# Pooled attention and a GELU MLP on one core: a step's loads placed behind its softmax transposes

## The chip, the cores and the metric

The kernel runs on one core of a Trainium2 chip. The metric is the device time of one execution in microseconds (us). The engines have names in the profile: PE is TensorE (matrix products; PEld is its loading of weights), DVE is VectorE, ACT is ScalarE, POOL is GpSimd, and SP is SyncE, which here issues nearly all DMAs.

## The reference

Inputs are q, k, v of shape (8 batches, 8 heads, 576 positions, 64) in float32, and two weight matrices.

```python
k_p = k.reshape(B, H, 72, 8, D).mean(axis=3)     # v_p likewise: eight positions pooled to one
scores = q @ k_p.T / sqrt(D)                     # softmax over the 72 pooled positions
attn_out = softmax(scores) @ v_p
x = attn_out as (4608 tokens, 512)
h = x @ w_in                                     # 512 -> 2048
out = gelu_tanh(h) @ w_out                       # 2048 -> 512
```

## The kernel before, in words

The tokens are worked in nine groups. Groups 0 to 7 are the first 512 positions of each batch; group R (number 8) holds the last 64 positions of all eight batches and runs in the last place but one (`seq` is 0 to 6, R, 7). The weights are put into SBUF once, as bf16.

A prologue computes the attention of group 0, then the MLP of group 0 runs (`mlp_first`). After that there is one step for each further group, numbered n_ from 1 to 8. In step n_ TensorE runs the MLP of group g = seq[n_], and between its matmuls stands the attention of the next group, seq[n_+1]. The MLP has a hidden part (16 blocks of four 128x512 matmuls at L421 and L360, each followed by a Gelu on ScalarE at L424 and L362) and an output part (seven products of a Strassen form, 112 matmuls of 256 columns at L472). Four PSUM banks with the tag `mm` take the hidden blocks in turn. VectorE prepares sums of the Gelu outputs for the products (`g_sums`, L411 to L414).

The order is written out by hand. `at(hooks, s, f, ...)` puts a call at place s of the step's matmuls; the call is made before that matmul in program order. Places 0 to 63 are the hidden part, 64 to 175 the output part. Each engine runs its own instructions in program order and waits only for its data and buffers, so for SyncE a place says only what stands before and after a DMA in its queue.

For the attention of the next group, these are the pieces that the change and the prediction speak of:

- `load_kv` loads K (1 MB, L108, and a half chunk at L103), a half chunk of V (L101) and then V (1 MB, L108) into one of two `kv` buffers; its `parts` choose K with the half chunks (0) or V (1). `load_q` loads the queries of a group (1 MB, L120) into one of two `q_sb` buffers; for group R it loads 64 rows of each batch into `q_r` (L124), two batches a call.
- `pool` sums eight positions on VectorE (L147 to L149). `k_transpose_dma` transposes the pooled keys through a DMA (kTd from kvb, L199), and `k_spread` copies the result into a block form on VectorE (kbd from kTd, L90). `spread_v` does a like thing for the values on GpSimd (L169).
- `cast_q` makes bf16 queries (q_b), and `q_transpose_dma` transposes them through a DMA (qT, L220). `cast_gated` does the casts on GpSimd behind a small copy from `eb`, which holds them back until the softmax weights of the step are written.
- `scores` (L236) at places 68 and 94, `exps` on ScalarE (L245), `norm` on VectorE, once on GpSimd (L252 to L267), and for each of four quarters an `e_transpose_dma` (eT from eb, L294) follow. `values` (L326; L335 for group R) at place 64 + 105 needs all four eT and gives the xT of the next step's MLP.
- `store_pair` writes half of a group's output (512 KB, L392) after the sixth and the seventh product.

In step n_ before the change, SyncE has, in order: kTd, the loads of K and V for the group two ahead, the q of that group, in steps 2 to 5 a part of group R's queries, four eT, a store, qT of the group two ahead, a store. Step 1 differs: its q for group 3 and K for group 3 are loaded at places 44 and 45, and V at 64 + 52, behind the fourth eT.

Of the kernel before, what the change touches and what calls it, by code (L numbers as in the profile page):

```python
# [19 lines left out]
def kernel(  # L20
# [21 lines left out]
    nc = tc.nc  # L42
# [10 lines left out]
    R = B  # L53
    seq = list(range(B - 1)) + [R, B - 1]
# [55 lines left out]
    def q_tile(g):  # L110
        if g < B:
            st[g]["q"] = work.tile([128, H, 4, D], F32, name="q_sb")
        else:
            st[g]["q"] = consts.tile([128, H, 4, D], F32, name="q_r")

    def load_q(g, j0, j1, eng):
        t = st[g]["q"]
        if g < B:
            src = q[g, :, :MAIN, :].rearrange("h (p j) d -> p h j d", j=4)
            eng.dma_start(out=t[:, :, j0:j1], in_=src[:, :, j0:j1])  # L120
        else:
            for b in range(2 * j0, 2 * j1):
                p0 = 64 * (b % 2)
                eng.dma_start(out=t[p0:p0 + 64, :, b // 2, :], in_=q[b, :, MAIN:, :].rearrange("h t d -> t h d"))  # L124
# [532 lines left out]
    def at(hooks, s, f, *a):  # L657
        hooks.setdefault(s, []).append(lambda: f(*a))
# [6 lines left out]
    hooks = {}  # L665
# [44 lines left out]
    for n_, g in enumerate(seq):  # L710
        if n_ == 0:
            continue
        hooks = {}
        if n_ == 1:
            for i in range(1, 4):
                at(hooks, i, w_sums, i, 0, NP, nc.vector)
            at(hooks, 36, g_sums, 0, 4)
        else:
            at(hooks, 20, g_sums, 0, 2)
            at(hooks, 36, g_sums, 2, 4)  # L720
        at(hooks, 57, g_sums, 4, 6)
        at(hooks, 65, g_sums, 6, 8)
        if n_ + 1 < len(seq):
            n = seq[n_ + 1]
            b = B - 1 if n == R else n
            kv = n != B - 1
            if n_ == 1:
                for j in range(4):
                    at(hooks, 28 + 4 * j, cast_q, n, j, j + 1, nc.scalar)
                at(hooks, 41, qT_tile, n)  # L730
                at(hooks, 41, q_transpose_dma, n)
            if kv:
                t0 = 22 if n_ == 1 else 12
                at(hooks, t0, pool, b, 0, 5)
                at(hooks, t0, dup_k, b, 0, 5)
                at(hooks, t0, kT_tile, b, None)
                at(hooks, t0, k_transpose_dma, b)
                t1 = t0 + (16 if n_ == 1 else 24)
                at(hooks, t1, pool, b, 5, 9)
                at(hooks, t1, spread_v, b, nc.gpsimd)  # L740
                at(hooks, 56, k_spread, b, [nc.vector, nc.vector])
            for j in range(4):
                if j % 2 == 0:
                    for f in (scores, exps):
                        for i in (j, j + 1):
                            at(hooks, 64 + (4 if j == 0 else 30), f, n, i)
                if j == 0:
                    at(hooks, 64 + 17, eT_tile, n)
                nj = 64 + [17, 33, 40, 50][j]
                at(hooks, nj, norm, n, j, nc.gpsimd if j == 1 else nc.vector)  # L750
                at(hooks, nj, e_transpose_dma, n, j)
            at(hooks, 64 + 66, nc.scalar.preload_act_table_set, GELU_SET)
            at(hooks, 64 + 105, xT_tile, n)
            at(hooks, 64 + 105, values, n, [nc.scalar, nc.vector])
        if n_ + 2 < len(seq):
            n2 = seq[n_ + 2]
            if n2 != R:
                s2 = 44 if n_ == 1 else 57
                at(hooks, s2, q_tile, n2)
                at(hooks, s2, load_q, n2, 0, 4, nc.sync)  # L760
            at(hooks, 64 + 52, cast_gated, n2)
            at(hooks, 64 + 100, qT_tile, n2)
            at(hooks, 64 + 100, q_transpose_dma, n2)
            if n_ == 1:
                at(hooks, 45, load_kv, n2, (0,))
                at(hooks, 64 + 52, load_kv, n2, (1,))
            else:
                at(hooks, 28, load_kv, n2)
        if n_ == 1:
            at(hooks, 58, q_tile, R)  # L770
        if 2 <= n_ <= 5:
            at(hooks, 58, load_q, R, n_ - 2, n_ - 1, nc.sync)
        mlp(g, hooks, n_ + 1 == len(seq))


# [28 lines left out]
```

The softmax here doesn't subtract the row's maximum and nothing guards it: scores larger than these inputs give would overflow.

## Time and profile before

| | us |
|---|---|
| median of 3 runs (284.69 to 285.91) | 285.53 |
| the profiled execution | 289.0 |
| its span, from the first to the last instruction | 287.3 |
| TensorE busy in that span | 276.0 |
| VectorE, ScalarE, GpSimd busy | 200.2, 168.2, 58.1 |

| step (by its hidden part's first matmul, L421) | starts at, us |
|---|---|
| 1 | 52.3 |
| 2 | 82.7 |
| 3 | 113.3 |
| 4 | 142.9 |
| 5, 6, 7, 8 | 171.3, 199.7, 228.8, 257.0 |

The times in a line of the profile are in us from the start of the span unless it says ns. A timeline's line gives the start, the length, the engine, the source line, the operation and the tiles written and read (`out<-in`), how many instructions are merged, and in brackets the idle time of the engine before the first of them with what ended it. A line of the windows view gives a stretch, its length, the busy time and count of instructions for PE, PEld, DVE, ACT and POOL, and at the end the granted TensorE clock (1 is full), the busy share of the DMA engines and GB/s. "DMA to landing" is the time from the start of the issuing instruction to the arrival of the data.

### The profile page before, as it was taken

To read this page: it belongs to the slowest core of one execution; us is meant where nothing else is said; L and a number is where in the kernel's file an instruction comes from. 1 tells how busy PE (TensorE), PEld (TensorE's weight loads), DVE (VectorE), ACT (ScalarE), POOL (GpSimd) and SP (SyncE) were. 2 spreads that over 40 slices of the span, in tenths; PEclk is the share of its full clock that TensorE was granted. 3 is DMA by queue.
4 is the path that set the end of the run, shared out by engine and by line. 5 is a ranking of instruction groups with operands and counts; after the bars stand their busy time and mean duration, and the time that the engine had idled before them with its cause. 6 is when DMAs were issued, how large, how long until landed. Compare 5 with 4: busy or idle time off the path is not lost.

```text
span 287.3 us, 6029 instructions
## 1 busy us (share of the span) xinstructions
PE 276.0 (96%) x2430; PEld 176.4 (61%) x2430; DVE 200.2 (70%) x361; ACT 168.2 (59%) x264; POOL 58.1 (20%) x91
## 2 busy tenths in 40 slices
PE   8889999998989997999999999999999999999994
PEld 3678844446844683448745864586458845864583
DVE  4882868987867984499679966996699435844521
ACT  1586574787446852676467646763776377637620
POOL 4740272002400340031203120312031200100000
PEclk9999999999999998999999999999999999999999
DMA  7999999999989998696689868946813730253013
GB/s 227 303 186 281 373 385 179 325 328 258 197 236 255 308 175 192 216 347 73 157 221 349 131 158 222 283 55 154 235 48 43 168 104 0 48 119 75 1 40 111
DMA packets 71759, 54.34 MB, mean 189 GB/s; under 512 B 45618, under 2 KB 57906, under 8 KB 71730
## 3 DMA queue, kind: packets, MB, share of 16 engines
q1 hardware_dynamic: 69474, 51.72, 70.2%
q0 software_dynamic: 2112, 2.10, 4.6%
q8 instruction: 19, 0.31, 0.5%
q10 hardware_dynamic: 144, 0.13, 0.1%
q14 instruction: 10, 0.08, 0.1%
HBM read 36.70 MB, written 9.44 MB: 161 GB/s over the span
## 4 chain that ended last, share of the span: by engine, by line
PE 78%; DMA 4%; DVE 3%; issue 1%
PE mm L360 32%; PE mm L472 31%; PE mm L421 5%; PE xo L326 3%; PE x L472 2%; DMA eT<-eb 2%; PE sc L236 2%; DMA qT<-q_b 2%; DVE eb L267 1%; DVE den L252 1%; PE xo L335 1%; PE mm L376 0%; DVE r L261 0%; DVE kv L147 0%; DVE kv L148 0%
## 5 line engine op out<-in xcount | busy, mean ns | idle before, releaser
L360 PE MATMUL mm<-xT,w_in_b 128*128 128x512 bf16 x448 | 98.0, 379 | 0.0
L362 ACT ACTIVATE gT<-mm 128x512 bf16<-128x512 f32 x112 | 66.9, 598 | 27.8 <-PE mm L360 27.7
L360 PEld LDWEIGHTS <-w_in_b 128*128 128x128 bf16 x448 | 43.7, 98 | 52.9
L472 PEld LDWEIGHTS <-gT 128*128 128x128 bf16 x512 | 48.5, 98 | 10.4 <-issue 2.5
L169 POOL TENSOR_TENSOR vbd<-kvb,vmask 128x256 bf16<-128x256 bf16 (+2 forms) x40 | 23.0, 597 | 96.6 <-DVE kvb L149 55.7
L472 PEld LDWEIGHTS <-stage 128*128 128x128 bf16 x384 | 37.5, 98 | 4.4
L411 DVE TENSOR_TENSOR stage<-gT 128x512 bf16<-128x512 bf16 (+1 forms) x31 | 15.6, 503 | 21.4 <-ACT gT L362 21.2
L472 PE MATMUL mm<-tw,gT 128*128 128x256 bf16 x240 | 30.4, 276 | 0.0
L472 PE MATMUL mm<-w_out_b,gT 128*128 128x256 bf16 x240 | 29.9, 273 | 0.0
L88 ACT CAST xT<-xo 128x1024 bf16<-128x1024 f32 (+1 forms) x11 | 10.2, 935 | 32.7 <-PE xo L326 28.0
L252 DVE TENSOR_REDUCE den<-e 128x8 f32<-128x576 f32 x36 | 26.5, 736 | 3.2 <-ACT e L245 2.9
L88 ACT COPY osb<-mm 128x512 f32<-128x512 f32 x30 | 17.6, 588 | 17.3 <-PE mm L472 17.0
L472 PE MATMUL mm<-tw,stage 128*128 128x256 bf16 x224 | 26.7, 273 | 0.0
L147 DVE TENSOR_TENSOR kv<-kv 128x1024 f32<-128x1024 f32 (+3 forms) x19 | 21.3, 1119 | 7.6 <-DMA kv<-in_k_dram 5.1
L245 ACT ACTIVATE e<-sc 128x576 f32<-128x576 f32 x36 | 21.8, 649 | 6.0 <-PE sc L236 4.4
L267 DVE TENSOR_TENSOR eb<-e,r 128x576 bf16<-128x576 f32 x25 | 20.8, 831 | 0.9
L412 DVE TENSOR_TENSOR gT<-gT 128x512 bf16<-128x512 bf16 (+1 forms) x31 | 14.6, 470 | 8.9 <-ACT gT L362 7.6
L90 DVE CAST xT<-xo 128x1024 bf16<-128x1024 f32 (+1 forms) x9 | 10.0, 1106 | 15.0 <-PE xo L326 11.4
L267 POOL TENSOR_TENSOR eb<-e,r 128x576 bf16<-128x576 f32 x7 | 8.1, 1150 | 56.5 <-ACT e L245 56.5
L90 POOL CAST q_b<-q_sb 128x1024 bf16<-128x1024 f32 (+1 forms) x13 | 13.6, 1067 | 20.1 <-DMA q_sb<-in_q_dram 20.0
L421 PE MATMUL mm<-xT,w_in_b 128*128 128x512 bf16 x64 | 16.3, 400 | 0.1
L371 PE MATMUL mm<-xT,w_in_b 128*128 128x256 bf16 x128 | 15.6, 273 | 0.1
(84 smaller groups left out, 288.9 us busy)
## 6 DMA issues: line engine op xcount, KB each, us to landing
kv<-in_k_dram SPq DMA_DIRECT2D x7, 1024.0 KB, 6.7
q_sb<-in_q_dram SPq DMA_DIRECT2D x7, 1024.0 KB, 11.3
kv<-in_v_dram SPq DMA_DIRECT2D x6, 1024.0 KB, 9.4
out_dram<-osb SPq DMA_DIRECT2D x12, 512.0 KB, 3.0
kv<-in_v_dram SPq DMA_DIRECT2D x4, 512.0 KB, 10.8
w_in_b<-in_moe_w_in_dram POOLq DMA_DIRECT2D x4, 512.0 KB, 6.7
w_out_s<-in_moe_w_out_dram SPq DMA_DIRECT2D x2, 1024.0 KB, 13.7
stage<-in_moe_w_out_dram SPq DMA_DIRECT2D x2, 1024.0 KB, 14.9
```

The source lines that it names most:

```text
L88: eng.copy(out=out, in_=in_)
L90: eng.tensor_copy(out=out, in_=in_)
L147: add(out=t[:, :, 0:4, :], in0=t[:, :, 0:4, :], in1=t[:, :, 4:8, :], op=ALU.add)
L169: eng.tensor_tensor(out=vbd[p0:128, b, n0:n1, :].rearrange("p (c r) (hh d) -> p c (r hh) d", c=max(m, 1), d=D), in0=kvb[p0:128, 4 + c0:4 + ...
L245: nc.scalar.activation(out=e.rearrange("p (x h) s -> p x (h s)", x=2), in_=sc[:, :, 0:4 * Sp], func=ACT.Exp, scale=1.0 / 64.0)
L252: nc.vector.reduce_sum(out=den, in_=e, axis=AX.X)
L267: eng.tensor_tensor(out=o.rearrange("p (pr hh s) -> p hh pr s", hh=2, s=Sp), in0=e.rearrange("p (hh pr) s -> p hh pr s", hh=2), in1=r.rear ...
L360: nc.tensor.matmul(out=hp, lhsT=w_in_b[:, ko, fo * 128:(fo + 1) * 128], rhs=st[g]["xT"][:, ko, :], start=(i == 0), stop=(i == KO - 1))
L362: nc.scalar.activation(out=gT[:, fo, :], in_=hp, func=ACT.Gelu_apprx_tanh)
L371: nc.tensor.matmul(out=hp[:, f, :], lhsT=w_in_b[:, ko, (fo + f) * 128:(fo + f + 1) * 128], rhs=st[g]["xT"][:, ko, c0:c0 + 256], start=(ko ...
L421: nc.tensor.matmul(out=hp[f], lhsT=w_in_b[:, ko, f * 128:(f + 1) * 128], rhs=st[g]["xT"][:, ko, :], start=(ko == 0), stop=(ko == 3))
L472: nc.tensor.matmul(out=xs[p] if acc is xs else acc[:, p, :], lhsT=lt, rhs=rt, start=bool(fresh and m == 0 and (p == 0 or (last and acc is ...
```

## The change

In each step the loads are placed behind the fourth eT (place 64 + 50) instead of ahead of the first. V is loaded for the group two ahead, as before, at place 64 + 53. K with the half chunks and q are loaded at 64 + 54 for the group three ahead, one group further than before. Group R's queries move to the same place and begin one step earlier, in steps 1 to 4. In step 1, K for group 3 stays at place 45, and q for group 3 moves from place 44 to 64 + 53. The queries of group 3 are cast in step 2 by ScalarE at places 16, 20, 24 and 28 and transposed at 29; before, GpSimd cast them in step 1 and they were transposed at its place 64 + 100. Later groups are cast and transposed where they were. SyncE then has in a step: kTd, four eT, V, K and half chunks, q, a part of group R's queries, a store, qT, a store.

```diff
-            if n_ == 1:
+            if n_ <= 2:
+                s0 = 28 if n_ == 1 else 16
                 for j in range(4):
-                    at(hooks, 28 + 4 * j, cast_q, n, j, j + 1, nc.scalar)
-                at(hooks, 41, qT_tile, n)
-                at(hooks, 41, q_transpose_dma, n)
+                    at(hooks, s0 + 4 * j, cast_q, n, j, j + 1, nc.scalar)
+                at(hooks, s0 + 13, qT_tile, n)
+                at(hooks, s0 + 13, q_transpose_dma, n)
...
+        def load_q_of(n):
+            q_tile(n)
+            load_q(n, 0, 4, nc.sync)
+
+        if n_ == 1:
+            at(hooks, 45, load_kv, seq[3], (0,))
         if n_ + 2 < len(seq):
             n2 = seq[n_ + 2]
-            if n2 != R:
-                s2 = 44 if n_ == 1 else 57
-                at(hooks, s2, q_tile, n2)
-                at(hooks, s2, load_q, n2, 0, 4, nc.sync)
-            at(hooks, 64 + 52, cast_gated, n2)
-            at(hooks, 64 + 100, qT_tile, n2)
-            at(hooks, 64 + 100, q_transpose_dma, n2)
+            at(hooks, 64 + 53, load_kv, n2, (1,))
             if n_ == 1:
-                at(hooks, 45, load_kv, n2, (0,))
-                at(hooks, 64 + 52, load_kv, n2, (1,))
+                at(hooks, 64 + 53, load_q_of, n2)
             else:
-                at(hooks, 28, load_kv, n2)
+                at(hooks, 64 + 52, cast_gated, n2)
+                at(hooks, 64 + 100, qT_tile, n2)
+                at(hooks, 64 + 100, q_transpose_dma, n2)
+        if n_ + 3 < len(seq):
+            n3 = seq[n_ + 3]
+            at(hooks, 64 + 54, load_kv, n3, (0,))
+            if n3 != R:
+                at(hooks, 64 + 54, load_q_of, n3)
         if n_ == 1:
-            at(hooks, 58, q_tile, R)
-        if 2 <= n_ <= 5:
-            at(hooks, 58, load_q, R, n_ - 2, n_ - 1, nc.sync)
+            at(hooks, 64 + 54, q_tile, R)
+        if 1 <= n_ <= 4:
+            at(hooks, 64 + 54, load_q, R, n_ - 1, n_, nc.sync)
```

## The prediction

> **What bounds the kernel now.** First the page: TensorE is busy nearly all the span, so only what makes it wait can move the time. Then TensorE's timeline in the steps that the diff touches. In its lines the number in brackets is the idle time before a group.
>
> ```profile
> PE 276.0 (96%) x2430; PEld 176.4 (61%) x2430; DVE 200.2 (70%) x361; ACT 168.2 (59%) x264; POOL 58.1 (20%) x91
> ```
>
> ```profile
> 67.51 0.46 PE L236 MATMUL sc<-kbd,qT 64*64 64x72 bf16 x32 [0.82 <-DMA qT<-q_b]
> ...
> 80.60 1.18 PE L326 MATMUL xo<-eT,vbd 32*64 32x512 bf16 x16 [1.02 <-issue]
> ...
> 110.87 1.18 PE L326 MATMUL xo<-eT,vbd 32*64 32x512 bf16 x16 [1.77 <-issue]
> ```
>
> From step 1 on these are the only holes: 0.82 us in step 1 (scores wait for the transposed queries), 1.02 at its end and 1.77 at the end of step 2 (the values wait for transposed softmax weights, eT). From step 3 on a step takes 28.4 us without a hole. After the third hole the windows view shows a second loss:
>
> ```profile
> 108.90:110.90 2.00, 0.23 (x6) 0.06 (x5) 0.00 (x0) 0.00 (x0) 0.00 (x0) 1.00 0.67 166
> 110.90:113.00 2.10, 2.10 (x22) 1.03 (x23) 0.89 (x1) 1.01 (x1) 0.00 (x0) 0.82 1.02 256
> 113.00:116.00 3.00, 3.00 (x11) 1.18 (x9) 2.93 (x4) 0.65 (x2) 0.00 (x0) 0.56 0.97 259
> ```
>
> The clock (third number from the end) falls to 0.82 and 0.56; the eight L421 matmuls take 2.88 us instead of 1.89 and the seven L472 before them 1.40 instead of 0.87, so 1.5 us are lost.
>
> Why eT is late is in SyncE's timeline, which issues nearly all DMAs in one order:
>
> ```profile
> 88.04 1.48 SPq L199 DMA_TRANSPOSE kTd<-kvb  x1
> 89.57 0.57 SPq L108 DMA_DIRECT2D kv<-in_k_dram  x1
> ...
> 92.04 0.51 SPq L120 DMA_DIRECT2D q_sb<-in_q_dram  x1
> 92.59 5.05 SPq L124 DMA_DIRECT2D q_r<-in_q_dram  x2
> 101.15 8.18 SPq L294 DMA_TRANSPOSE eT<-eb  x4
> ...
> 141.11 3.23 SPq L220 DMA_TRANSPOSE qT<-q_b  x1
> 144.44 0.54 SPq L392 DMA_DIRECT2D out_dram<-osb  x1
> 146.35 1.20 SPq L199 DMA_TRANSPOSE kTd<-kvb  x1
> ```
>
> The first eT of step 2 is issued at 101.15 and lands 6.1 us later, at 107.3, just after the rest queries (q_r, 106.7): it queued behind the step's loads. The kTd of 146.35, with nothing but a store ahead, lands in 2.6 us:
>
> ```profile
> L294 SPq DMA_TRANSPOSE eT<-eb x1: 3572/3572/3572, 101.2 to 101.2; - x1
> ...
> DMA to landing us min/median/max: 6.1/6.1/6.1
> ```
>
> ```profile
> L199 SPq DMA_TRANSPOSE kTd<-kvb x1: 1202/1202/1202, 146.4 to 146.4; - x1
> ...
> DMA to landing us min/median/max: 2.6/2.6/2.6
> ```
>
> **The Trainium skill.** "DMA: Bandwidth & Descriptors", section Queues, rings and completion order: a DMA engine takes the descriptors of one queue in ring order. The trace agrees (6.1 against 2.6 us). "TensorE: Matmul & The Clock Gate", section What's actually happening: the array's clock is halved after an idle window of some 3.4 us. The trace's clock record has half speed for 3.41 us from 112.24, and 1.77 us of idling inside a window was enough; 1.02 was not. The same page's table of the array calls ScalarE's queue strictly in order: a cast that waits holds back every Gelu behind it. No wait of this kind is in the trace before.
>
> **The change part by part.** All bytes and all DMAs stay; they move on SyncE's queue.
>
> *Off the path of eT.* In step 1 the 1 MB of q for group 3 no longer stands before eT. The K load then lands some 3 us earlier than 75.3, so the second eT (issued 74.29, taking 2.10) takes its usual 1.2 to 1.6, and the last one lands near 79.6 instead of 80.40: the hole of 1.02 goes. In step 2 nothing stands before eT: the third hole, 1.77, goes, and with it the half clock, 1.5. The 0.82 stays, as nothing before it moves. Profiled 289.0 (span 287.3 plus 1.7 around it) − 1.02 − 1.77 − 1.5 = **284.7**. The median, 285.53, lies 3.5 below the profiled execution, so the timed runs hardly pay these losses, and the gain against the median is at most about 0.8.
>
> *GpSimd and ScalarE.* Group 3's gate and two casts leave GpSimd (0.19 + 2 × 1.04 us; it is 20% busy: nothing). Four casts of 0.6 us go to ScalarE between Gelus of step 2. Step 1 has the same four at 59.0 to 62.6 and TensorE ran on through them, as four PSUM banks lie between: 0 in themselves. Their wait for q is counted below.
>
> *In the way of kTd and qT.* Behind the last eT now come, in one block, V, K with two half chunks, q and q_r, and only then store, qT, store and kTd (in step 2: both stores, kTd, qT). Before, the latter four came first. Scores need kTd, then k_spread on VectorE (0.93 us), and qT. Call X the start of the values matmuls; the last eT is issued 2.75 before, V 1.45 before, and scores of the next step are due at X + 16.4 (140.86 to 157.28).
>
> Two bounds on the block. *Lower*, by the packet records (median 84 ns for 2 KB, 46 for 1 KB, 18 for 256 B, 159 for 4 KB, over 16 engines): V 32 × 84 = 2.7 us, K with halves 40 × 84 = 3.4, q 64 × 46 = 2.9, q_r 64 × 18 = 1.2, a store 8 × 159 = 1.3, qT 128 × 18 = 2.3, kTd 40 × 18 = 0.7; data begins 2 us after the issue, and landing comes about 0.9 after the last packet. *Upper*, by the distance from one landing to the next in a full queue: the first V 6.8 after its issue, K 3.3, halves 1.2, q 3.9, q_r 1.0, store 1.3, qT 2.5, kTd 0.7 (K at 124.25 to q_r at 133.46 in step 3 is such a chain).
>
> - Steps 3 and 4 (3.5 MB loaded in the step before). Lower: X + 0.5 + 15.8 + 0.9 = X + 17.2, with k_spread 18.1: TensorE waits 1.7. Upper: 5.4 (V), 9.9 (K), 13.8 (q), 14.8, 16.1, 18.6, 19.9, 20.6 (kTd), 21.5: it waits 5.1. I take two thirds of the way up, since the mean packet (106 ns for 2 KB) is well over the median: 4.0 each, **8.0**.
> - Step 2 (4.5 MB; q of group 3 too). V issued about 78.2. Lower: 80.2 + 18.7 + 0.9 = 99.8; upper: 85.1, q3 89.0, K 93.5, q4 97.4, 98.4, stores 101.0, kTd 101.7, qT 104.2. Scores would be due at 96.1 (97.02 less the hole). Wait 3.7 to 8.1, taken **6.6**. ScalarE's casts, due about 85.5, wait for q3 until 87 to 89; the Gelus behind stall, the banks cover 3.5 us, and what is left (0 to 2.5) lies inside this wait, for qT comes later still.
> - Step 5 (2.5 MB, no q): 0 to 1.2, taken **0.8**. Step 6 (V and q alone): scores in time, VectorE late by up to 1.6; taken **0.3**.
> - What follows each wait of steps 2 to 4: an idle time above 1.77 should halve the clock again, 1.5 as measured. Should it not, VectorE is late instead: it waits in k_spread, then has eight sums of 0.46, so the softmax starts 3.75 after scores instead of 2.26 (97.02 to 99.28), and eT, which had 0.1 to spare in step 3 (landed 140.7, needed 140.8), comes 0.9 or more late. The one covers the other: 1.5 each, **4.5** (2.7 to 5.1).
>
> Sum: 284.7 + 8.0 + 6.6 + 0.8 + 0.3 + 4.5 = **304.9**; all lower ends 294.5, all upper ends 310. As the timed runs pay less for late transfers than the profiled one, I take **303**.
>
> **Rivals.**
> *Not slower: the block drains in time.* If transposes pass the loads, or the 3.5 MB land so fast that kTd lands before X + 15.5, only the holes go: 284.7, or 283.9 with the first hole gone too. For: the DMA engines are 0.72 to 0.87 busy in the windows of steps 4 and 5, so there is room over a step. Against: even the lower bound misses that point by 1.7, and every eT behind loads landed behind them. Chance 0.07.
> *Only ScalarE's wait.* kTd is in time, but the casts of step 2 hold TensorE for 1.3 to 2.5: 286 to 287. Chance 0.05.
> *Only step 2.* 4.5 MB are too much and 3.5 MB just fit: 284.7 + 3.7 + 1.5 = 290. Chance 0.08.
> *That the order isn't moved* is excluded: SyncE's list of instructions has V, K, q and q_r after the four eT in each step.
> The main case, waits for kTd in steps 2 to 4: 0.80.
>
> **Numbers.** Within 0.5% (1.4 us) is what a measurement of this kernel can tell from no change. Faster by more: 0.04, the larger part of the rival that drains in time (its first hole gone too). Same: 0.06, the rest of it (0.03) and of the second rival 0.03. Slower: 0.90, the main case, the third rival and the second's last 0.02. The main case's range is 294 to 310; to hold the time 8 times in 10 beside the third rival it reaches down to 292.
>
> **What would show it.** Right: in the profile after, TensorE's idle time before L236 in steps 2, 3 and 4 of several us, released by kTd or qT (k_spread on VectorE, the copy kbd<-kTd at L90, waiting for DMA kTd); kTd landing 9 us or more after its issue where it took 2.6; no idle time before L326 in steps 1 and 2; clock below 1 after each wait. Wrong: kTd landing in under 4 us, steps 3 and 4 still 28.4 us long, or the wait sitting at L360 behind ScalarE's casts.

## The result, and the profile after

The changed kernel takes 302.65 us (median of 6 runs, 300.83 to 303.82); before it is 285.52. The ratio is 1.0598, with a 95% interval of 1.0554 to 1.0642: 17 us slower, where 303 us was forecast. The profiled execution of the changed kernel took 303.72 us with a span of 302.0, so it lies 1.1 above its median. The profile before is of a slow execution (289.0 us, mean granted clock 0.992), while 64 of the 66 executions of that kernel timed beside the experiments have a clock of 0.997 or more, so its half clock is not part of the 17 us, which lie between the medians.

The page shows the same work in TensorE, now 92% of the span:

```profile
PE 277.7 (92%) x2412; PEld 178.2 (59%) x2430; DVE 196.4 (65%) x361; ACT 169.9 (56%) x268; POOL 54.4 (18%) x88
```

TensorE's timeline of the changed kernel, with the idle time before each group in brackets:

```profile
67.08 0.46 PE L236 MATMUL sc<-kbd,qT 64*64 64x72 bf16 x32 [0.69 <-DMA qT<-q_b]
...
79.24 1.18 PE L326 MATMUL xo<-eT,vbd 32*64 32x512 bf16 x16
...
102.57 0.70 PE L236 MATMUL sc<-kbd,qT 64*64 64x72 bf16 x32 [6.75 <-DMA qT<-q_b]
...
116.44 1.18 PE L326 MATMUL xo<-eT,vbd 32*64 32x512 bf16 x16
...
136.42 0.71 PE L236 MATMUL sc<-kbd,qT 64*64 64x72 bf16 x32 [3.49 <-DVE kbd L90]
...
169.24 0.71 PE L236 MATMUL sc<-kbd,qT 64*64 64x72 bf16 x32 [2.41 <-DVE kbd L90]
...
182.39 1.18 PE L326 MATMUL xo<-eT,vbd 32*64 32x512 bf16 x16 [0.60 <-DMA eT<-eb]
...
199.20 0.71 PE L236 MATMUL sc<-kbd,qT 64*64 64x72 bf16 x32 [0.32 <-DVE kbd L90]
...
212.40 1.18 PE L326 MATMUL xo<-eT,vbd 32*64 32x512 bf16 x16 [0.65 <-DMA eT<-eb]
```

Both holes that the change could take away are gone: the values matmuls (L326) at 79.24 and 116.44 start without a wait, where 1.02 and 1.77 us stood in the profile before. In their place scores (L236) wait 6.75, 3.49, 2.41 and 0.32 us in steps 2 to 5.

SyncE's timeline shows what the wait is made of:

```profile
107.21 6.74 SPq L294 DMA_TRANSPOSE eT<-eb  x4
114.00 0.58 SPq L108 DMA_DIRECT2D kv<-in_v_dram  x1
...
116.38 0.61 SPq L120 DMA_DIRECT2D q_sb<-in_q_dram  x1
117.04 3.95 SPq L124 DMA_DIRECT2D q_r<-in_q_dram  x2
121.09 3.35 SPq L392 DMA_DIRECT2D out_dram<-osb  x1
124.55 5.48 SPq L220 DMA_TRANSPOSE qT<-q_b  x1
130.12 0.53 SPq L392 DMA_DIRECT2D out_dram<-osb  x1
130.75 1.36 SPq L199 DMA_TRANSPOSE kTd<-kvb  x1
```

The block V to q_r now stands ahead of store, qT, store and kTd, and qT alone holds SyncE for 5.48 us. kTd is issued at 130.75; before the change it was issued 5.6 us after the values matmuls began (146.35 against 140.79), now 14.3 after (130.75 against 116.44). So of the 11.5 us by which kTd lands later after the values, 8.7 are a later issue, since SyncE itself is held by what stands ahead, and 2.8 a longer way from issue to landing (5.4 against 2.6). The view of line L199 in a window around it:

```profile
L199 SPq DMA_TRANSPOSE kTd<-kvb x1: 1358/1358/1358, 130.7 to 130.7; - x1
...
  DVE kbd L90: 6.2, 1
...
DMA to landing us min/median/max: 5.4/5.4/5.4
```

VectorE waits 6.2 us for it (kbd, L90) and TensorE for VectorE. After the waits of steps 2 and 3 the windows view (TensorE's clock is the third number from the end) shows the half clock:

```profile
102.50:106.60 4.10, 4.03 (x49) 2.98 (x50) 3.82 (x9) 1.78 (x3) 0.00 (x0) 0.51 0.00 0
...
...
136.40:140.70 4.30, 4.24 (x50) 3.08 (x50) 3.92 (x10) 1.78 (x3) 0.00 (x0) 0.60 0.00 0
```

The last two numbers of the first line are telling too: while TensorE runs at half clock behind the wait of step 2, the DMA engines move nothing at all.

### The profile page after: what moved, and what is told of

Same layout as the page of the kernel before. It is cut to its first block, busy times and chain, and to the rows that moved or that the text cites. A ratio compares the mean times of both kernels' runs of the same rounds, so it can differ in the third digit from the quotient of the medians.

```text
span 302.0 us, 6012 instructions
## 1 busy us (share of the span) xinstructions
PE 277.7 (92%) x2412; PEld 178.2 (59%) x2430; DVE 196.4 (65%) x361; ACT 169.9 (56%) x268; POOL 54.4 (18%) x88
## 4 chain that ended last, share of the span: by engine, by line
PE 73%; DMA 12%; DVE 8%; SPq 3%; issue 1%; ACT 1%; POOL 0%; DVEq 0%
PE mm L472 29%; PE mm L360 24%; DMA kTd<-kvb 5%; PE mm L421 5%; PE mm L371 5%; DMA qT<-q_b 4%; PE xo L326 3%; PE x L472 2%; PE sc L236 2%; SPq L220 2%; DMA eT<-eb 2%; DMA kv<-in_v_dram 2%; DVE den L252 1%; DVE eb L267 1%; PE mm L376 1%
## 5 line engine op out<-in xcount | busy, mean ns | idle before, releaser
L360 PE MATMUL mm<-xT,w_in_b 128*128 128x512 bf16 x440 | 97.7, 379 | 0.4
L472 PEld LDWEIGHTS <-gT 128*128 128x128 bf16 x512 | 50.1, 101 | 12.2 <-issue 2.9
L169 POOL TENSOR_TENSOR vbd<-kvb,vmask 128x256 bf16<-128x256 bf16 (+2 forms) x40 | 21.9, 570 | 99.9 <-DVE kvb L149 93.9
L245 ACT ACTIVATE e<-sc 128x576 f32<-128x576 f32 x36 | 22.1, 650 | 22.1 <-PE sc L236 18.3
L472 PE MATMUL mm<-w_out_b,gT 128*128 128x256 bf16 x240 | 33.2, 293 | 0.0
L411 DVE TENSOR_TENSOR stage<-gT 128x512 bf16<-128x512 bf16 (+1 forms) x31 | 14.5, 469 | 21.7 <-ACT gT L362 21.5
L236 PE MATMUL sc<-kbd,qT 64*64 64x72 bf16 x512 | 8.3, 202 | 13.9 <-DMA qT<-q_b 7.4
L412 DVE TENSOR_TENSOR gT<-gT 128x512 bf16<-128x512 bf16 (+1 forms) x31 | 13.7, 441 | 8.8 <-ACT gT L362 7.6
L90 DVE CAST xT<-xo 128x1024 bf16<-128x1024 f32 (+1 forms) x9 | 10.0, 1106 | 14.0 <-PE xo L326 10.5
L90 DVE COPY kbd<-kTd 64x288 bf16<-64x288 bf16 x12 | 3.5, 291 | 22.1 <-DMA kTd<-kvb 21.9
L236 PEld LDWEIGHTS <-qT 64*64 64x64 bf16 x512 | 6.3, 111 | 18.0 <-DMA qT<-q_b 10.4
```

What stands on the lines that cost most here:

```text
L169: eng.tensor_tensor(out=vbd[p0:128, b, n0:n1, :].rearrange("p (c r) (hh d) -> p c (r hh) d", c=max(m, 1), d=D), in0=kvb[p0:128, 4 + c0:4 + ...
L236: nc.tensor.matmul(out=sc[p0:p0 + 64, hh, Sp * pr:Sp * pr + Sp], lhsT=qT[h0:h0 + 64, j, pr, p0:p0 + 64], rhs=kbd[h0:h0 + 64, g if g < B el ...
L245: nc.scalar.activation(out=e.rearrange("p (x h) s -> p x (h s)", x=2), in_=sc[:, :, 0:4 * Sp], func=ACT.Exp, scale=1.0 / 64.0)
L360: nc.tensor.matmul(out=hp, lhsT=w_in_b[:, ko, fo * 128:(fo + 1) * 128], rhs=st[g]["xT"][:, ko, :], start=(i == 0), stop=(i == KO - 1))
L472: nc.tensor.matmul(out=xs[p] if acc is xs else acc[:, p, :], lhsT=lt, rhs=rt, start=bool(fresh and m == 0 and (p == 0 or (last and acc is ...
```

## The experiments

The theory was that kTd and qT stand behind too many bytes, and that this alone makes the 17 us. The rivals: ScalarE's casts of group 3, the order of SyncE's queue whatever the bytes, and engines that are full whatever the queue.

**e1: the block goes back behind kTd.** One part is undone:

```diff
-        if n_ + 3 < len(seq):
-            n3 = seq[n_ + 3]
-            at(hooks, 64 + 54, load_kv, n3, (0,))
+        if 2 <= n_ and n_ + 2 < len(seq):
+            n3 = seq[n_ + 2]
+            at(hooks, 30, load_kv, n3, (0,))
             if n3 != R:
-                at(hooks, 64 + 54, load_q_of, n3)
+                at(hooks, 30, load_q_of, n3)
...
-        if 1 <= n_ <= 4:
-            at(hooks, 64 + 54, load_q, R, n_ - 1, n_, nc.sync)
+        if 2 <= n_ <= 5:
+            at(hooks, 30, load_q, R, n_ - 2, n_ - 1, nc.sync)
```

> The changed kernel, with K, q and q_r of the block moved from behind the last eT to place 30 of the next step, so behind kTd and, in step 2, behind qT; V stays behind the last eT, and group 3 is still cast by ScalarE in step 2. Theory (kTd and qT stand behind 3.5 to 4.5 MB in one queue): only 1 MB (2 MB in step 1) stands before them, TensorE's idle time before L236 in steps 2 to 4 (6.75, 3.49, 2.41 us) falls under 0.5 us each, and so does the half clock that followed; about 285 us, up to 288 if the loads of step 2 now hold its eT as before the change. Rival (ScalarE's casts of step 2 and their wait for q hold the step): step 2 keeps several us of waiting, over 292.

Measured: 286.58 us, 1.0046 of before (1.0029 to 1.0063). Of the 17 us, 16 are gone. TensorE's timeline has no wait before scores in steps 2 to 5, and kTd lands 3.3 us after its issue:

```profile
95.74 0.45 PE L236 MATMUL sc<-kbd,qT 64*64 64x72 bf16 x32
...
107.10 1.14 PE L472 MATMUL mm<-tw,gT 128*128 128x256 bf16 x9 [0.27 <-DVE osb L457]
108.98 1.18 PE L326 MATMUL xo<-eT,vbd 32*64 32x512 bf16 x16 [0.73 <-issue]
...
125.40 0.45 PE L236 MATMUL sc<-kbd,qT 64*64 64x72 bf16 x32
```

```profile
L199 SPq DMA_TRANSPOSE kTd<-kvb x1: 1493/1493/1493, 115.9 to 115.9; - x1
...
DMA to landing us min/median/max: 3.3/3.3/3.3
```

So the place of K, q and q_r is the cause, not V's place, nor ScalarE's casts, which are still there. The half per cent that stays has a visible part, 0.27 + 0.73 us at the end of step 2: qT of group 3 waits for ScalarE's casts and is issued at 90.29, the loads follow at 91.84 instead of 89.57, and eT of that step meets them, as before the change.

**e2: fewer bytes, same order.** Three loads of 1 MB, the q of groups 4, 5 and 6, leave the blocks ahead of steps 2, 3 and 4; these groups then work on the queries of group 3.

```diff
-            if n3 != R:
+            if n3 in (4, 5, 6):
+                at(hooks, 64 + 54, lambda n3=n3: st[n3].__setitem__("q", st[3]["q"]))
+            elif n3 != R:
                 at(hooks, 64 + 54, load_q_of, n3)
```

> The changed kernel without the 1 MB loads of q for groups 4, 5 and 6; these groups work on the queries of group 3 instead. All else stays in its order. Theory (the wait is the bytes ahead in the queue): each block ahead of steps 2, 3 and 4 is some 3.3 us shorter, so TensorE waits before L236 about 3.4, 0.2 and 0 us instead of 6.75, 3.49 and 2.41; the half clock of step 3 (1.9) and what followed in step 4 (0.6) go; 291 us, 289 if step 2 keeps full clock. Step 5, whose block had no q, keeps its 0.3 and 0.65. Rival (it is the order and SyncE's issuing of transposes, whatever the bytes): 300 to 303.

Measured: 290.68 us, 1.0183 of before (1.0149 to 1.0218), 12 below the changed kernel.

```profile
97.82 0.45 PE L236 MATMUL sc<-kbd,qT 64*64 64x72 bf16 x32 [1.96 <-DMA qT<-q_b]
...
126.54 0.71 PE L236 MATMUL sc<-kbd,qT 64*64 64x72 bf16 x32 [0.23 <-DVE kbd L90]
...
139.68 1.18 PE L326 MATMUL xo<-eT,vbd 32*64 32x512 bf16 x16 [0.60 <-DMA eT<-eb]
...
156.17 0.71 PE L236 MATMUL sc<-kbd,qT 64*64 64x72 bf16 x32
```

The waits go from 6.75, 3.49 and 2.41 to 1.96, 0.23 and none: by 4.8, 3.3 and 2.4, against the 3.3 expected for 1 MB (the last had no more to lose; why the first lost more stays open). In the profiled execution, 289.92 us, the clock stays full; the other three have a mean clock of 0.994, as one stretch of half clock would give, so part of the median is that. The wait follows the bytes. What remains is instructive: in steps 3 to 5 scores hardly wait, yet 0.6 us stand before L326, which fits VectorE coming late out of k_spread and eT with it (no run takes that apart).

**e3: the same block on another queue.** GpSimd issues it, at the same places:

```diff
-            at(hooks, 64 + 53, load_kv, n2, (1,))
+            if n_ == 1:
+                at(hooks, 64 + 53, nc.gpsimd.tensor_copy, gate, eb[:, 3, 639:640])
+            at(hooks, 64 + 53, load_kv, n2, (1,), nc.gpsimd)
...
-            at(hooks, 64 + 54, load_kv, n3, (0,))
+            at(hooks, 64 + 54, load_kv, n3, (0,), nc.gpsimd)
...
-            at(hooks, 64 + 54, load_q, R, n_ - 1, n_, nc.sync)
+            at(hooks, 64 + 54, load_q, R, n_ - 1, n_, nc.gpsimd)
```

(`load_q_of` too.) The small copy in step 1 holds GpSimd's first loads behind the last softmax weights, as the copy in `cast_gated` does in later steps.

> The changed kernel with the same loads (V, K with half chunks, q, q_r of steps 1 to 5) issued by GpSimd's queue at the same places instead of SyncE's; step 1 has one more small copy on GpSimd that holds them behind the last softmax weights. The same bytes move at about the same time. Theory (order in one queue): kTd and qT no longer stand behind the loads, kTd lands within 4 us of its issue and the waits before L236 fall under 1 us each: 284 to 290. Rival (the DMA engines themselves are full just then, whatever the queue): kTd and qT take 5 us or more to land and the waits stay above half: 295 or more. Open: GpSimd's own time for issuing, which could delay its casts and vbd products.

Measured: 306.34 us, 1.072 of before (1.0659 to 1.078). The theory as it stood, that order in one queue alone makes the transposes late, is refuted; its rival, that they are late whatever the queue, is right for this pair of queues. SyncE's timeline, and the view of L220 for one qT:

```profile
105.78 6.01 SPq L294 DMA_TRANSPOSE eT<-eb  x4
113.11 0.33 SPq L392 DMA_DIRECT2D out_dram<-osb  x1
114.02 13.57 SPq L220 DMA_TRANSPOSE qT<-q_b  x1
...
128.27 4.91 SPq L199 DMA_TRANSPOSE kTd<-kvb  x1
```

```profile
L220 SPq DMA_TRANSPOSE qT<-q_b x1: 13575/13575/13575, 114.0 to 114.0; - x1
...
DMA to landing us min/median/max: 20.5/20.5/20.5
```

In SyncE's queue only a store stands ahead of this qT, and still it takes 20.5 us to land (5.1 before the change) and holds SyncE for 13.57. It lands at 134.5, just after the last load of GpSimd's block (133.4). The Trainium skill, "DMA: Bandwidth & Descriptors", section Queues, rings and completion order, says that each DMA engine takes turns between its queues packet by packet. The trace agrees, if its packet records may be taken for those turns. From 120 to 129 us, when both queues have work, the DMA view counts (packets, MB, share of the 16 engines; q0 is GpSimd's queue, q1 SyncE's):

```profile
q0 software_dynamic: 622, 2.27, 95.7%
q1 hardware_dynamic: 604, 0.15, 12.9%
```

Nearly one for one: but a packet of qT has 256 B, and one of the loads 4 KB (896 packets for the 3.5 MB), so qT gets 0.15 MB through while the loads get 2.27. On SyncE's queue the same loads go in packets of 2 KB, 1 KB and 256 B, so e3 changed the packets together with the queue; another queue with the small packets was not run. And kTd, which took 8.0 us to land here, stands behind qT in SyncE's queue, so only qT shows what traffic beside it does.

The waits before scores in steps 3 and 4 are 6.83 and 3.36 us. In step 2 there is none; the loss came before it: in step 1 GpSimd's block started at 76.41, the same moment as the fourth eT, where SyncE's queue would have kept it behind, and the values matmuls waited 4.15 us.

**e4: GpSimd casts group 3.**

```diff
-                    at(hooks, s0 + 4 * j, cast_q, n, j, j + 1, nc.scalar)
+                    at(hooks, s0 + 4 * j, cast_q, n, j, j + 1, nc.scalar if n_ == 1 else nc.gpsimd)
```

> The changed kernel with the four casts of group 3 in step 2 made by GpSimd instead of ScalarE, at the same places; SyncE's order is the same. Theory: ScalarE's wait for q3 (1.15 us) lies inside the wait for kTd and qT, so the time stays within 1.5 us of 302.7. Rival (ScalarE's casts and their wait cost step 2 its time): faster by 2 us or more.

Measured: 302.70 us, 1.0585 of before (1.0548 to 1.0622): the same as the changed kernel. In its profile scores of step 2 wait 5.01 us instead of 6.75 (qT is issued at 93.76 instead of 94.97), but the medians do not show it: ScalarE's casts cost nothing that can be told.

**b1 to b3: how much may stand behind eT?** They start from the kernel before. b1 moves V alone; b2 also takes q_r out of step 2; b3 also moves K of group 3 in step 1.

```diff
@@ b1 @@
             else:
-                at(hooks, 28, load_kv, n2)
+                at(hooks, 28, load_kv, n2, (0,))
+                at(hooks, 64 + 53, load_kv, n2, (1,))
@@ b2 @@
-        if 2 <= n_ <= 5:
-            at(hooks, 58, load_q, R, n_ - 2, n_ - 1, nc.sync)
+        if 3 <= n_ <= 5:
+            at(hooks, 58, load_q, R, n_ - 3, n_ - 2 if n_ < 5 else 4, nc.sync)
@@ b3 @@
             if n_ == 1:
-                at(hooks, 45, load_kv, n2, (0,))
-                at(hooks, 64 + 52, load_kv, n2, (1,))
+                at(hooks, 64 + 52, load_kv, n2)
```

> The kernel before with one part of the change: in steps 2 to 5 only V (1 MB) moves behind the last eT; K, q and q_r stay ahead of the first eT, group 3 is treated as before. Theory (what counts is how many bytes stand between two groups of transposes, 3.5 MB ahead of eT before the change, 3.5 MB ahead of kTd after it): 2.5 MB ahead of eT land some 3 us earlier in step 2, so the 1.77 us hole there goes, and 1 MB ahead of kTd delays it by some 3 us, of the 5 that it had; step 1 keeps its hole of about 1 us. 284.3 to 285.5, same to 0.4% faster than before. Rival (anything heavy behind eT costs): a wait before L236 in steps 3 to 6, over 288.

> As b1, and q_r (0.25 MB) leaves step 2: its parts are loaded in steps 3, 4 and two in step 5. Theory: step 2, where the DMA engines are fullest, gets 1 us more of room; 284 to 285.3, not above b1 by more than 0.3. Rival: step 5 with 0.5 MB of q_r holds its eT: 0.5 to 1 us slower than b1.

> As b2, and in step 1 K with its half chunks for group 3 moves from ahead of eT to behind it, ahead of V. Theory: eT of step 1 finds an empty queue, the hole of about 1 us there goes; kTd of step 2 lands near 92 instead of 91 and scores (due 96) do not wait; loads of step 2 end about 103, so its eT may be 0.5 late: 283.5 to 285. Rival: 2.25 MB ahead of qT and kTd in step 2 already make scores wait: over 286.

Measured against before (285.25 us in these runs): b1 284.81, ratio 0.9982 (0.9967 to 0.9996); b2 285.04, 0.9986 (0.9970 to 1.0003); b3 285.34, 0.9996 (0.9978 to 1.0013). b1 is 0.2% below the kernel before, at the edge of what can be told; the other two cannot be told from before. b1's timeline keeps only the holes of step 1:

```profile
67.49 0.45 PE L236 MATMUL sc<-kbd,qT 64*64 64x72 bf16 x32 [0.96 <-DMA qT<-q_b]
80.72 1.18 PE L326 MATMUL xo<-eT,vbd 32*64 32x512 bf16 x16 [1.15 <-DMA eT<-eb]
...
109.15 1.18 PE L326 MATMUL xo<-eT,vbd 32*64 32x512 bf16 x16
```

In b2 0.50 us stand before the values of step 2 where b1 has none, so the room that q_r was to leave there does not show. In b3 the hole before the values of step 1 is gone as expected, but 0.27 and 0.67 us stand at the end of step 2: the bytes moved, and the wait with them.

## Why the prediction was right, point by point

- *Off the path of eT: 1.02, 1.77 and 1.5 go.* Right for the profile. L326 starts without a wait in steps 1 and 2, and what was left to gain against the median was small, as said: b1, which clears step 2 alone, gets 0.4 us.
- *GpSimd and ScalarE: nothing.* Right. ScalarE waited 1.15 us for q3, as its timeline has it (a cast at 86.72), TensorE did not stop in the hidden part, and e4 took the casts away from ScalarE without effect on the median.
- *Step 2: 6.6.* Measured 6.75, with qT landing at 102.53 where the bounds were 99.8 and 104.2.
- *Steps 3 and 4: 4.0 each.* Measured 3.49 and 2.41: the term that was mis-sized, by 2.1 in sum. It can be read off: V was put 1.45 us ahead of the values matmuls, but in the steps after a half clock TensorE is slower, eT gets ahead of it, and V was issued 2.44 and 2.19 ahead (114.00 against 116.44; 148.16 against 150.35). And scores start once the first half of k_spread is written and follow kTd's landing by 0.3 us (136.11 to 136.42), not by 0.93. These two make 3.0; against them the block took 1.1 longer in sum, 22.1 us in step 3 from V's issue to kTd's landing and 20.8 in step 4, where 20.9 each was taken. As for the bounds, the packet records have the first packets 1.2 to 1.4 us after the issue of a load (V at 79.08, K at 117.69 and 147.61) and a landing at most 0.6 after the last one (q at 120.16), not 2 and 0.9: the lower bound stood about 1 us too high. (The 28.4 us of a step before hold for steps 4 and 5; step 3, with the half clock, took 29.6.)
- *Step 5: 0.8; step 6: 0.3.* Measured 0.32 before scores and 0.65 before L326 in step 5, none in step 6.
- *After each wait 1.5, by half clock or by late eT.* Near in sum, and right in kind, with luck in the sum. From the first to the second group of scores step 2 took 5.19 us and step 3 5.25, against 3.34 in step 1: 1.9 each. In step 4 the clock stayed full, although 2.41 us of idling is above the 1.77 that was taken to be enough, and eT came late instead: 0.25 in that stretch and 0.60 before L326, so about half of the 1.5. Together 4.6 against 4.5. Which steps get the half clock could not have been told from the length of their waits (last section).
- *The sum.* The measured terms, 6.75 + 3.49 + 2.41 + 0.97 + 4.6 = 18.2, on 284.7 give 302.9; the profiled execution took 303.72, so 0.8 is not assigned (0.25 of it is step 5's scores, which took 3.59 us from the first to the second group). The prediction had 20.2 and then took off 2 for the timed runs; the timed median lies 1.1 below the profiled one. That 303 stands within 0.4 of 302.65 is therefore luck in part: the terms were 2.0 too high, and this was met by the 0.8 that is not assigned and by 0.9 too much taken off.
- *What would show it.* The idle time before L236, the releasers and the free L326 of steps 1 and 2 came as listed. Two signs did not: kTd was to land 9 us or more after its issue and took 8.4, 5.4 and 4.5 in steps 2 to 4, and the clock was to fall after each wait, which it did not in step 4. The first says where the delay sits: the prediction had kTd waiting behind the loads after its issue, but most of the delay was before it, with SyncE held by the DMAs ahead (8.7 of 11.5 us in step 3).
- *The mechanism as it was put* was that a transpose behind loads in one queue waits for them. That is how it was in this kernel, but e3 shows that one queue is not needed for it: beside the same loads from GpSimd's queue qT is later still. The rival "drains in time" would not have come true by that change of queue. The forecast did not depend on this, since the change keeps one queue.

## What to carry to other kernels

When loads are moved out from ahead of one latency-bound transfer, ask which is the next one behind them and how long the block takes to land: here 3.5 MB took some 15 us from the first issue to the last landing (114.00 to 129.28), and there were two groups of transposes in each step to be kept clear of it, so what fits is a split (V behind eT, the rest behind kTd), not a move. In this kernel a transpose of small packets needed a time of little traffic, and taking the loads to another queue did not replace it. And where TensorE is 96% busy the gain of such a move is bounded by the holes in its timeline (a few us in the profile, under 1 in the median), while its loss is not.

## What was not expected of the hardware

A DMA transpose holds its issuing engine longer when loads are under way: issuing qT took SyncE 3.0 us in step 1 of the changed kernel, 5.5 behind the blocks of steps 1 and 2, 8.65 behind V and q at the end of step 5, and 13.57 beside loads from another queue (e3), with everything behind it in the queue held too.

An idle time of TensorE does not halve its clock by its length alone. 1.77 us did before the change, and 2.30 in step 4 of e4; 2.41 in step 4 of the changed kernel, 2.96 in step 3 of e4 and 1.96 in e2 did not. The traces show what decides. In each of the nine, the times at which the clock changes lie whole multiples of 3.413 us apart, so time is cut into fixed windows of that length. These stretches are such windows, two of the kernel before and three of the changed one (step 4). Behind the stretch stand its length and TensorE's busy time; the clock is the third number from the end:

```profile
108.83:112.24 3.41, 1.64 (x22) 0.55 (x20) 0.15 (x2) 0.35 (x1) 0.00 (x0) 1.00 0.76 207
112.24:115.65 3.41, 3.41 (x13) 1.57 (x11) 3.34 (x4) 1.25 (x2) 0.00 (x0) 0.50 1.01 233
...
164.58:167.99 3.41, 2.26 (x13) 1.11 (x12) 0.00 (x0) 2.73 (x4) 1.50 (x4) 1.00 1.07 222
167.99:171.40 3.41, 2.12 (x46) 1.81 (x46) 2.20 (x7) 1.54 (x3) 0.00 (x0) 1.00 0.14 32
171.40:174.82 3.42, 3.42 (x61) 2.88 (x60) 3.18 (x8) 1.24 (x2) 0.00 (x0) 1.00 0.00 0
```

The 1.77 us before the change lie in one window, and the next has half clock. The 2.41 of step 4 fall on two windows, 1.15 and 1.29 idle, and the clock stays full. From 60 us to 8 us before the end, the nine traces have 577 such windows: each of the 11 with 1.77 us or more of idle time in it is followed by half clock, and none of those with 1.62 or less is. So a hole of some 2 us is followed by half clock when enough of it falls into one window, and by none when it is split between two; its length alone does not tell which.
